# A four-layer linear-attention and MLP kernel: the first loads cut anew, two K projections split by weight halves, and a new order for the first layer

## The chip, the cores and the metric

The kernel runs on one core of a Trainium2 chip. The metric is the device time of one execution in microseconds. A page of the profile and a trace exist for one profiled execution, whose own time is given beside its span (first to last instruction of the program). All times inside the span are in microseconds from its start.

The engines are named as in the profile: PE is TensorE (matmuls and transposes; PEld is its weight load), ACT is ScalarE, DVE is VectorE, POOL is GpSimd, SP is SyncE, which issues the DMAs.

## The reference

Two kinds of layer run in turn, A, B, A, B, with the same weights both times. The sequence has 2048 tokens of width 512, in bfloat16.

```python
x = x + A(layernorm(x), wqkv, wo)   # 32 heads of 16
x = x + B(layernorm(x), w1, w2)     # 512 -> 1376 -> 512, relu
x = x + A(layernorm(x), wqkv, wo)
x = x + B(layernorm(x), w1, w2)

# A: linear attention
phi = lambda t: where(t > 0, t + 1, exp(t)) + 1e-6
pq, pk = phi(q), phi(k)
kv  = einsum("bhsd,bhse->bhde", pk, v);  z = pk.sum over s
num = einsum("bhqd,bhde->bhqe", pq, kv)
den = einsum("bhqd,bhd->bhq", pq, z) + 1e-6
A   = (num / den) @ wo
# B
B   = relu(x @ w1) @ w2
```

## The kernel before

The 2048 tokens are 16 tiles of 128, four tiles to a chunk. Every layer is written as a list of operations (`g.add`), each with its engine, what it reads and writes, and an assumed duration. A list scheduler in the kernel's own Python, `_list_schedule`, then fixes the order on each engine when the kernel is built. It takes the operations by priority: their place in the list, shifted by a table `HINTS`. The table `SEQS` forces the order of a few operations of the first layer on each engine, and `STT` names the steps that use a fused VectorE form. The engines run their lists strictly in order, with waits on semaphores, so the order is fixed and the chip decides only the times. PSUM banks (8) are also given out by the scheduler; an operation that takes a bank waits for the one that read it last.

The first layer, where all of the change lies, runs as follows. Names are those of the scheduler; `i` is a tile.

- SP issues the loads in this order: `ld_x0_0` (tile 0, 128 KB), `ld_x0_1` (tiles 1 to 3, 384 KB), `ld_wk0` and `ld_wk1` (the two halves of the K weights by contraction rows, 256 KB each), `ld_x1_0` (chunk 1, 512 KB), `ld_wq` (the Q weights, 512 KB), the chunks 2 and 3, then the V weights and `wo`.
- Warm-up: TensorE runs nine 512-column matmuls on zeros (`warm`, L451) and one of 256 columns (`warm2`, L454).
- Chunk 0: statistics `bnst`/`bnag` on VectorE (L476, L477); tile 3 has its mean and square sum from ScalarE (`mean_3`, `sq_3`, L890, L892). VectorE subtracts the mean (`cent`, L880). TensorE transposes the centred tile in four 128-column steps (`trp`, L549) and ScalarE or VectorE copies the result out of PSUM (`trev`, L553, L554). For tile 0 both are cut in halves (`trp0a`, `trp0b`). The division by the standard deviation is left to the evacuation of the projections (scale `rstd`, made on GpSimd: `veps`, `rstd`, L874, L876). `norm0` to `norm3` (L925) make the normalised tiles for the later K-transposed-x products.
- Chunk 1: statistics, `veps` and `rstd` for two tiles at a time, `norm4` to `norm7` (L515), transposes on TensorE (`trp4` to `trp7`).
- Chunks 2 and 3: the same, but transposed by DMA (`tr2_0`, `tr2_1`, `tr3_0`, L532).
- `kproj` is the K projection of one tile, four 512-column matmuls (one for each 128 rows of contraction); `qtok` is the Q projection of a tile of chunk 0, `qproj1_0` and so on those of the other chunks. Each is followed by `lin` and `exp` on ScalarE (L576, L578) and `em` and `phi` on VectorE (L580, L587; fused form L584). `g` are the products of K and normalised x, in 256 or 512 columns, which accumulate over all tiles. All of them are matmuls of L594.
- Then `zcol`, `kv` and `m` fold the V and output weights in; `den` (four matmuls of 32 output rows) gives the denominators, `lnd` and `rdc` their inverse on ScalarE, `spread` copies them out by DMA, `pqs` multiplies Q by them (L748), and `fin` is the output projection, with `resid` (L605) adding it to x.

In `a_k`, only tile 0's K projection is split by the two halves of its weights:

```python
for c0, n, key, tag in ((0, 2, "T0a", "a"), (2, 2, "T", "b")) if i == 0 and g.layer == 0 else ((0, 4, "T", ""),):
```

`FIRST_ORDER = (0, 3, 1, 2)` is the order in which the list has the tiles of chunk 0.

## Time and profile before

| | |
|---|---|
| median of 3 runs | 281.06 us (280.62 to 281.25) |
| the profiled execution | 281.25 us, span 279.5 us |
| PE busy | 275.4 us, 99% of the span |
| ACT, DVE, POOL busy | 172.5, 141.6 and 47.1 us |
| DMA | 22.62 MB, mean 81 GB/s over the span |
| first matmul (warm-up), first transpose, first K projection | 1.24, 5.05, 5.95 us |
| first transpose of chunk 1 | 13.68 us |

In the timeline, a row has the start, the time that the merged instructions span, the engine, the line, the operation, what it writes and reads, the shape and the count; in brackets stands the idle time before them and what ended it. Matmuls overlap in the array, so the spacing of starts, not the duration of one, is what a matmul costs. In the table by stretches, the columns are the stretch, its length, the busy time of PE, PEld, DVE, ACT and POOL (with the number of instructions), the granted clock, the busy share of the DMA engines and GB/s. In the chain, a row has the start and the length of a piece.

### The profile page before, as it was taken

To read this page: it belongs to the slowest core of one execution; us is meant where nothing else is said; L and a number is where in the kernel's file an instruction comes from. 1 tells how busy PE (TensorE), PEld (TensorE's weight loads), DVE (VectorE), ACT (ScalarE), POOL (GpSimd) and SP (SyncE) were. 2 spreads that over 40 slices of the span, in tenths; PEclk is the share of its full clock that TensorE was granted. 3 is DMA by queue.
4 is the path that set the end of the run, shared out by engine and by line. 5 is a ranking of instruction groups with operands and counts; after the bars stand their busy time and mean duration, and the time that the engine had idled before them with its cause. 6 is when DMAs were issued, how large, how long until landed. Compare 5 with 4: busy or idle time off the path is not lost.

```text
span 279.5 us, 4209 instructions
## 1 busy us (share of the span) xinstructions
PE 275.4 (99%) x1573; PEld 140.6 (50%) x1573; DVE 141.6 (51%) x381; ACT 172.5 (62%) x355; POOL 47.1 (17%) x126
## 2 busy tenths in 40 slices
PE   8999999999999999999999999999999999999996
PEld 3455656546554544544454455674554554454443
DVE  5899983899501362353353477379935300120222
ACT  4999797748864583578372799766884366226000
POOL 6500000044500170300040400003236100000000
PEclk9999999999999999999999999999999999999999
DMA  6913388654630053070004030075331641011012
GB/s 202 379 54 64 75 227 267 150 140 76 133 58 0 2 93 76 1 96 0 0 1 77 0 75 2 0 182 122 76 71 26 160 83 21 0 70 26 0 75 75
DMA packets 46356, 22.62 MB, mean 81 GB/s; under 512 B 36640, under 2 KB 44800, under 8 KB 46336
## 3 DMA queue, kind: packets, MB, share of 16 engines
q1 hardware_dynamic: 46336, 22.35, 33.9%
q8 instruction: 12, 0.20, 0.3%
q14 instruction: 8, 0.07, 0.1%
HBM read 7.14 MB, written 2.10 MB: 33 GB/s over the span
## 4 chain that ended last, share of the span: by engine, by line
PE 94%; DMA 2%; DVE 2%; SPq 1%; issue 0%
PE ps L594 94%; DMA xin<-in_A_x_dram 2%; DVE bst L476 1%; PE ps L549 0%; SPq L426 0%; SPq L420 0%; DVE xn L515 0%; DVE mv L477 0%; DVE xin L843 0%; DVE escr L580 0%; DVE veps L483 0%
## 5 line engine op out<-in xcount | busy, mean ns | idle before, releaser
L594 PE MATMUL ps<-w,big 128*128 128x512 bf16 (+3 forms) x363 | 77.5, 373 | 0.0
L594 PE MATMUL ps<-Tb,w 128*128 128x512 bf16 (+1 forms) x352 | 70.8, 360 | 0.0
L823 ACT ACTIVATE big<-ps 128x512 bf16<-128x512 f32 x71 | 42.3, 597 | 23.7 <-PE ps L594 23.4
L594 PEld LDWEIGHTS ps<-w,big 128*128 128x128 bf16 (+1 forms) x363 | 35.1, 98 | 41.2 <-ACT big L823 0.3
L594 PEld LDWEIGHTS ps<-Tb,w 128*128 128x128 bf16 x352 | 34.0, 98 | 32.8
L611 ACT ACTIVATE sqscr<-xres 128x512 bf16<-128x512 f32 x48 | 29.9, 625 | 31.1 <-DVE xres L605 30.8
L605 DVE SCALAR_TENSOR_TENSOR xres<-ps,xres 128x512 f32<-128x512 f32 x32 | 21.2, 690 | 42.6 <-PE ps L594 42.6
L602 DVE TENSOR_TENSOR xin<-ps,xres 128x512 bf16<-128x512 f32 x15 | 10.4, 691 | 49.7 <-PE ps L594 49.7
L576 ACT ACTIVATE big<-ps 128x512 bf16<-128x512 f32 x51 | 31.9, 628 | 5.0 <-PE ps L594 5.0
L594 PE MATMUL ps<-wqkv,Tb 128*128 128x512 bf16 x144 | 33.5, 381 | 0.0
L594 PE MATMUL ps<-big,xn 128*128 128x256 bf16 (+1 forms) x224 | 30.6, 288 | 0.0
L578 ACT ACTIVATE escr<-ps 128x512 bf16<-128x512 f32 x44 | 27.8, 636 | 1.0 <-PE ps L594 1.0
L594 PE MATMUL ps<-Tb,wqkv 128*128 128x512 bf16 x112 | 26.5, 379 | 0.0
L594 PEld LDWEIGHTS ps<-big,xn 128*128 128x128 bf16 x224 | 21.6, 98 | 8.6 <-issue 0.4
L594 PE MATMUL ps<-Mf,big 128*128 128x512 bf16 x112 | 25.2, 379 | 0.0
L580 DVE TENSOR_SCALAR escr<-escr 128x512 bf16<-128x512 bf16 x52 | 14.9, 293 | 18.0 <-ACT escr L578 17.7
L497 POOL TENSOR_SCALAR mean<-s 128x4 f32<-128x4 f32 x12 | 3.0, 247 | 119.0 <-DVE xres L605 118.8
L594 PEld LDWEIGHTS ps<-wqkv,Tb 128*128 128x128 bf16 x144 | 13.8, 98 | 16.0 <-ACT Tb L553 0.3
L587 DVE TENSOR_TENSOR big<-big,escr 128x512 bf16<-128x512 bf16 x49 | 20.5, 423 | 1.1
L524 ACT ACTIVATE xn<-xres,nbias,rstd 128x512 bf16<-128x512 f32 x15 | 12.0, 816 | 9.4 <-POOL nbias L509 9.4
L594 PEld LDWEIGHTS ps<-Mf,big 128*128 128x128 bf16 x112 | 10.8, 98 | 13.2 <-DVE big L748 0.5
L519 DVE TENSOR_SCALAR xn<-xres,mean,rstd 128x512 bf16<-128x512 f32 x23 | 15.2, 690 | 4.0 <-POOL nbias L509 3.9
(94 smaller groups left out, 226.2 us busy)
## 6 DMA issues: line engine op xcount, KB each, us to landing
big<-rdc SPq DMA_DIRECT2D x32, 128.0 KB, 2.7
xin<-in_A_x_dram SPq DMA_DIRECT2D x3, 512.0 KB, 8.1
w<-in_B_w_dram SPq DMA_DIRECT2D x1, 1376.0 KB, 8.3
w<-in_B_w_dram SPq DMA_DIRECT2D x1, 1280.0 KB, 10.9
wqkv<-in_A_wqkv_dram SPq DMA_DIRECT2D x2, 512.0 KB, 8.5
out_dram<-xin SPq DMA_DIRECT2D x2, 512.0 KB, 2.8
wqkv<-in_A_wqkv_dram SPq DMA_DIRECT2D x2, 256.0 KB, 3.8
wo<-in_A_wo_dram SPq DMA_DIRECT2D x1, 512.0 KB, 8.9
```

What stands on the lines that cost most here:

```text
L497: g.add(POOL, lambda e: e.tensor_scalar(mean[:, sl], s1[:, sl], -INV_D, None, ALU.mult), [("s1", i) for i in tl], [("mean", i) for i in tl ...
L519: ts = (POOL, lambda e: e.tensor_scalar(xn[:, i, :], src, mean[:, i:i + 1], rstd[:, i:i + 1], ALU.add, ALU.mult), C_POOL_NORM)
L524: (ACT, lambda e: e.activation(xn[:, i, :], src, ACTF.Identity, scale=rstd[:, i:i + 1], bias=nbias[:, i:i + 1]), C_ACT_SB_AP)],
L576: g.add(ACT, lambda e: e.activation(dst_ap, psv[:, b, :], ACTF.Identity, bias=1.0 + 1e-6, scale=sc), [("ps", b)] + rk, [dst_key], C_ACT_PS ...
L578: g.add(ACT, lambda e: e.activation(esc, psv[:, b, :], ACTF.Exp, scale=sc), [("ps", b)] + rk, [ekey], C_ACT_EXP + xd, name=name + "_exp")
L580: g.add(DVE, lambda e: e.tensor_scalar(esc, esc, 1.0, 1e-6, ALU.min, ALU.add), [ekey], [ekey], C_DVE_BF4X, name=name + "_em")
L587: g.add(DVE, lambda e: e.tensor_tensor(dst_ap, dst_ap, esc, ALU.max), [dst_key, ekey], [dst_key], 340.0, name=name + "_phi")
L594: last = e.matmul(o, l, r, start=st, stop=sp, skip_group_check=skip)
L602: g.add(DVE, lambda e: e.tensor_tensor(xin[:, i, :], psv[:, b, :], src, ALU.add), [("ps", b), skey], [("xin", i)], C_DVE_PSUM, name="resid ...
L605: g.add(DVE, lambda e: e.scalar_tensor_tensor(xres[:, i, :], psv[:, b, :], 0.0, src, ALU.add, ALU.add, accum_out=s1[:, i:i + 1]), [("ps", ...
L611: g.add(ACT, lambda e: e.activation(sqscr[:, q, :], xres[:, i, :], ACTF.Square, accum_out=s2[:, i:i + 1]), [("xres", i)], [("sqscr", q), ( ...
L823: g.add_flex([(ACT, lambda e, M=M, b=b, u=u: e.activation(unit_ap(u, M), psv[0:M, b, :], ACTF.Relu), C_ACT_PSUM), (DVE, lambda e, M=M, b=b ...
```

## The change

- The load of tiles 1 to 3 becomes two: tile 1 (128 KB), then tiles 2 and 3 (256 KB).
- The load of chunk 1 becomes two: tiles 4 and 5 (256 KB) ahead of the Q weights, tiles 6 and 7 behind them.
- The warm-up has eight matmuls instead of nine, and the 256-column one is gone.
- `FIRST_ORDER` is (0, 1, 3, 2), and the K projections of its first two tiles, 0 and 1, are split by the halves of their weights.
- `HINTS`, `SEQS` and `STT` are new for the first layer, and the scheduler assumes 218 ns for a group of denominators, and twice 95 ns more where it does not follow another one.

What the scheduler makes of it on TensorE, from the first transposes on:

```text
before: trp0a warm2 trp0b kproj0a trp3 trp2 kproj0b trp1 kproj3 kproj2 kproj1 qtok0 qtok3 qtok1
        trp4 trp5 qtok2 kproj4 trp6 trp7 kproj5 kproj6 kproj7 qproj1_0 qproj1_1 qproj1_2 qproj1_3 ...
after:  trp0a trp0b kproj0a trp3 trp2 trp1 kproj0b kproj2 kproj3 qtok0 qtok1 qtok3 qtok2
        trp4 trp5 kproj1a kproj1b kproj4 trp6 trp7 kproj5 kproj6 qproj1_1 kproj7 qproj1_0 qproj1_2 qproj1_3 ...
```

On VectorE, `bnst1` now stands ahead of `cent0`, and `trev2` and `trev1` come from ScalarE; on ScalarE, `trev3` stands ahead of `sq_3`, and `trev7` comes from VectorE in the place of `trev5`, which goes there. The denominators stand on TensorE as `den0 den2`, `den1`, `den3` before, each group between other matmuls, and as `den0`, `den2`, `den1`, `den3` after. `pqs1_3` follows `pqs1_2` directly on VectorE instead of standing behind `resid9`. The order of the later layers stays, but for the first matmul groups of the second layer, where `h0_0_0` now stands ahead of `hr0_1`. TensorE runs two matmuls fewer (one of the warm-up and the 256-column one); all else has the same number of them.

```diff
-    "dve": ["bnst0", "bnag0", "cent0", "bnst2", "bnst1", "bnag2", "cent3", "bnag1", "cent2", "trev0b"],
-    "act": ["mean_3", "trev0a", "sq_3", "trev3", "trev2", "trev1"],
-    "pool": ["veps_0", "rstd_0", "veps_2", "veps_1", "rstd_1", "var_3"],
-    "pe": ["trp0a", "warm2"],
+    "dve": ["bnst0", "bnag0", "bnst1"],
+    "act": ["mean_3", "trev0a", "trev3", "sq_3", "k0_exp", "k3_exp", "q0_0_lin", "k2_exp"],
+    "pool": ["veps_0", "rstd_0", "veps_2", "nm2_3"],
+    "pe": ["trp0a", "trp0b", "kproj0a", "trp2", "trp1"],
 }
-STT = {"0.k10", "0.k6", "0.k9", "0.q3_2", "0.q3_3"}
+STT = {"0.k13", "0.k5"}
...
         o.t_start = st
+        if o.key.startswith("0.den"):
+            o.dur = C_DEN if order[PE][-1].name.startswith("den") else C_DEN + 2 * C_MM_SWITCH
...
-                 WARM=9, SPLIT0=True, TAIL_SPLIT=True, LAST_HALVES=True, FIRST_PE_CHUNKS=2,
+                 WARM=8, SPLIT0=True, TAIL_SPLIT=True, LAST_HALVES=True, FIRST_PE_CHUNKS=2,
...
         ld_x(0, 0, 1, 100.0)
-        ld_x(0, 1, lat=1550.0)
+        ld_x(0, 1, 2, 550.0)
+        ld_x(0, 2, 4, 950.0)
...
-        ld_x(1, lat=1450.0)
-        dma(lambda e: e.dma_start(wqkv[:, :, 0:D], wq_v[:, :, 0:D]), [], [("wq",)], 1550.0, "ld_wq")
+        ld_x(1, 0, 2, 900.0)
+        dma(lambda e: e.dma_start(wqkv[:, :, 0:D], wq_v[:, :, 0:D]), [], [("wq",)], 1600.0, "ld_wq")
+        ld_x(1, 2, 4, 850.0)
...
-            g.add(PE, lambda e: e.matmul(psv[:, wt, 0:256], wrm[:, 0:128], wrm[:, 0:256], start=True, stop=True),
-                  [("wrm",)], [("ps", wt)], 213.0, name="warm2")
...
-            for c0, n, key, tag in ((0, 2, "T0a", "a"), (2, 2, "T", "b")) if i == 0 and g.layer == 0 else ((0, 4, "T", ""),):
+            for c0, n, key, tag in ((0, 2, "T0a" if i == 0 else "T", "a"), (2, 2, "T", "b")) if i in FIRST_ORDER[:2] and g.layer == 0 else ((0, 4, "T", ""),):
...
-        FIRST_ORDER = (0, 3, 1, 2)
+        FIRST_ORDER = (0, 1, 3, 2)
```

## The prediction

> **What bounds the kernel now.** I read the page first (busy time, then the chain), next the chain in order of time, then the timeline of each engine over the first 17 us, and last the DMA view narrowed to one issue at a time.

> ```profile
> PE 275.4 (99%) x1573; PEld 140.6 (50%) x1573; DVE 141.6 (51%) x381; ACT 172.5 (62%) x355; POOL 47.1 (17%) x126
> PE 94%; DMA 2%; DVE 2%; SPq 1%; issue 0%
> ```

> TensorE carries the chain, so a change pays only where TensorE starts later than it could, waits, or runs slowly. The chain names the one load that still sets a start:

> ```profile
> 2.69 6.34 DMA xin<-in_A_x_dram
> ...
> 13.31 0.33 DVE xn L515
> 13.64 0.04 issue
> 13.68 0.72 PE ps L549 x8
> ```

> Chunk 1 of x lands at 2.69 + 6.34 = 9.03; its statistics and norms lead to transposes `trp4` and `trp5` at 13.68. What TensorE did meanwhile (start, us, instructions):

> ```profile
> 5.05 0.42 PE L549 MATMUL ps<-ident,xn 128*128 128x128 bf16 x2
> 5.26 0.42 PE L454 MATMUL ps<-wrm 128*128 128x256 bf16 x1
> 5.48 0.42 PE L549 MATMUL ps<-ident,xn 128*128 128x128 bf16 x2
> 5.95 0.84 PE L594 MATMUL ps<-wqkv,Tb 128*128 128x512 bf16 x2
> 6.73 0.72 PE L549 MATMUL ps<-ident,xn 128*128 128x128 bf16 x8
> 7.30 0.59 PE L594 MATMUL ps<-wqkv,Tb 128*128 128x512 bf16 x2
> 7.73 0.39 PE L549 MATMUL ps<-ident,xn 128*128 128x128 bf16 x4
> 7.95 5.34 PE L594 MATMUL ps<-wqkv,Tb 128*128 128x512 bf16 x24
> 13.68 0.72 PE L549 MATMUL ps<-ident,xn 128*128 128x128 bf16 x8 [0.39 <-DVE xn L515]
> ```

> The nine warm-up matmuls stand 0.43 us apart; at 5.95 a 512-column matmul still takes 0.40; from 7.30 on it is 0.216 ((5.34 - 0.38)/23). The 24 at 7.95 would hand over at 7.95 + 24 x 0.216 = 13.13; the next start is 13.68, so chunk 1 costs 0.55. From there to 277.1 TensorE is dense. The wait list of its matmuls has 0.4 us beside the start, so nothing else large can be won.

> **The change, part by part.** All times below are of the profiled execution: 281.25 with a span of 279.5 (1.75 outside it). The runs' median is 281.06, 0.19 lower.

> *Start.* One warm-up matmul (0.43) and the filler (0.21) go: TensorE is free at 1.24 + 8 x 0.427 = 4.65. VectorE now does `bnst1` ahead of `cent0`: 3.65 + 0.08 + 0.58, so `cent0` runs at 4.33 and ends at 4.68 (it was 3.87 to 4.22). Tile 1's load is the 128 KB issued second at 1.25; with the 2.1 us of the first load it lands at 3.36, in time. Transposes: 4.74 to 5.17, four at 0.107. ScalarE's `mean_3` starts when tiles 2 and 3 are in (512 KB as before; 4.45 to 4.6) and holds ScalarE 0.63, so `trev0a` starts at 5.2 and ends at 5.6; `kproj0a` starts 0.06 later, at 5.67 instead of 5.95, if `wk0` is in. `wk0` landed at 1.71 + 3.6 = 5.3 with the same bytes ahead; one more issue (0.47) makes it 5.3 to 5.6. Two matmuls at 0.40, then three transposes (`trp3`, `trp2`, `trp1`, 0.22 each; VectorE has the last centred tile at about 6.2) and `kproj0b` (0.43): `kproj2` starts at 7.60. In the old order the same work was over at 7.95: 0.35 gained. `trev2` moves to VectorE, 7.15 to 7.56, just in time.

> *Between 7.6 and chunk 1.* Before, 4 K projections and 3 Q projections ran ahead of `trp4`; now `kproj1` goes behind it and `qtok2` ahead of it: the same count. `kproj2` and `kproj3` end at 7.60 + 8 x 0.216 = 9.33; then `qtok0` wants the Q weights. These landed at 3.20 + 7.27 = 10.47, just ahead of their use at 10.54. Now 256 KB of chunk 1 go behind them. How early that makes them depends on a dip of the loads:

> ```profile
> 5.50:6.50 1.00, 0.95 (x5) 0.26 (x3) 0.81 (x4) 0.99 (x3) 0.00 (x0) 1.00 0.98 240
> 6.50:7.50 1.00, 1.00 (x11) 0.56 (x10) 0.97 (x5) 0.33 (x2) 0.89 (x3) 1.00 0.76 284
> ...
> 9.00:10.50 1.50, 1.50 (x8) 0.59 (x6) 1.45 (x4) 1.50 (x4) 0.52 (x1) 1.00 1.03 414
> ```

> (The last column is GB/s.) Late end: the dip stays, 262 KB at 414 GB/s are 0.63, so 9.84; with a little for shorter rows 9.9. Early end: the two slow stretches run at about 390, as 7.5 to 9 did, which is 0.26 MB or 0.65 us more: 9.2. No row decides, since the dip stands where the 4 KB rows of chunk 1 begin and these become 2 KB; I take the middle, 9.55. TensorE then waits 0.21 at `qtok0`, and the 16 matmuls of four Q projections end at 9.55 + 3.45 = 13.0, against 13.68: 0.68 gained (0.33 at the late end, 0.89 at the early one).
> [...]

> *Is chunk 1 ready by 13.0?* Its first half lands by 8.4 and its second half by 10.5 to 10.6 (the byte place that the Q weights had). VectorE: `bnst6`, `bnst7` 10.63 to 11.82, `norm4` 11.9 to 12.3, `norm5` to 12.6. `rstd4` on GpSimd needs 0.8 after `veps4` at about 10.4. So `trp4` is ready 0.7 ahead, `trp5` too (its 0.09 wait of the old order goes), and `kproj1` between `trp5` and `kproj4` covers `trev4` (0.5 on ScalarE). The stall of 0.55 is gone; late next is the Q weights.

> *13 to 44 us.* ScalarE was idle 0.17 us between 14.4 and 29.6, so TensorE's bank waits hang on it. Its list there changes little: two transposes' evacuations fewer and one more (0.49 each), `sq_3` (0.61) moved from idle time at 5.8 to behind `trev3`. Laying its operations end to end (0.57 with a scale per token, 0.48 without) against TensorE at 0.216, each release comes 0.2 to 0.6 us ahead of need; the thinnest are `q1_0_exp` before `g0_3_0` and `q0_3_lin` before `kproj8`. `tr3_0` leaves about 1 us later than at 29.35, but `kproj12` comes at 35 instead of the old first use at 33.7. Three steps fewer use the fused VectorE form, so ScalarE has three more `lin` (0.48 each): one between 26 and 38, where it idles 0.8, 0.5 and 0.65, and two (`q3_2`, `q3_3`) between 45 and 52, where it idles 0.4, 0.3 and 1.1. I cost this at nothing; if the cover fails, each late release costs its own lateness.

> *Denominators.* Entering and leaving the 32-column matmuls costs about 0.1 each way:

> ```profile
> 45.18 0.40 PE L594 MATMUL ps<-xres,Zc 128*32 128x512 bf16 x4
> 45.41 0.39 PE L594 MATMUL ps<-big,Zc 128*32 128x512 bf16 x4
> 45.73 0.62 PE L594 MATMUL ps<-GT,wqkv 128*128 128x128 bf16 x8
> ```

> The second group starts 0.23 after the first, the one after it 0.31 later. `den0` and `den2` stood together (three blocks of denominators); now all four stand alone: 0.20 lost. Later `pqs1_3` no longer stands behind `resid9` (0.61) on VectorE, so the 0.14 that `fin4` waited at 60.5 goes. Layers 1 to 3 keep their order but for one pair at 67.9.

> Sum: 0.68 + 0.09 + 0.14 - 0.20 = 0.71, so 281.25 - 0.71 = 280.54. The median run stands 0.19 below the profiled one; part of that is likely a shorter stall at 13.68, so I take half: **280.45**.

> **The rivals.**
> (a) *The Q weights take over the stall.* At the late end (9.9) the gain is 0.33 + 0.09 + 0.14 - 0.20 = 0.36: 280.9, or 280.7 beside the median run. For it: the weights were only 0.07 ahead before. Against: in a run with less of the dip both waits shrink.
> (b) *The clock comes late: slower.* Full rate came about 5.2 us after the first matmul, between 5.95 and 6.73. The old order kept TensorE nearly busy till then (pause 5.69 to 5.95). The new one pauses 5.17 to 5.67, without the filler. If that pause restarts the count, full rate comes at 5.67 + 5.2 = 10.9; 4.4 us at half rate lose 2.2, and the wait for the Q weights vanishes under it: 281.25 - 0.92 + 2.2 = 282.5. It decides for slower if full rate comes later than about 9.1. Against: the old pause did no visible harm.
> [...]
> (c) *Something on the way to the matmuls is late*, above all ScalarE: if its four thinnest margins fail by 0.3 each, 1.2 is lost: 281.7. The dense 13.7 to 44.5 under an equally full ScalarE speaks against it.
> (d) *All is early*: Q weights at 9.2, no wait: 281.25 - 0.92, 280.3.

> **How the numbers follow.** About 0.2% (0.56 us) is what a measurement of this kernel can tell from no change: faster means below 280.5. The forecast with (d): 0.48, ending at 280.0 to 280.5. (a): 0.24, within 0.2%. (b): 0.15 and (c): 0.13, slower. The range takes in the forecast, (a), (d), (c) and the cheaper half of (b): 279.9 to 282.0.

> **What would show it.** Right: 512-column matmuls 0.216 apart by 7.2; `kproj0a` near 5.7; no idle time before L554 at about 13.0; idle time, if any, before `qtok0` with a release by the wqkv load. Wrong: matmuls 0.43 apart after 7, TensorE waiting on ScalarE between 14 and 30, or `trp4` still waiting for a norm at 13.7.

## The result, and the profile after

The changed kernel takes 282.31 us (median of 6 runs, 281.92 to 282.98), the kernel before beside it 280.95 (6 runs, 280.62 to 281.49): ratio 1.0049, interval 1.0032 to 1.0066. It is 1.36 us slower, 1.9 above the forecast and 0.3 outside the range. The profiled execution took 282.64 with a span of 280.9, so 1.4 more inside the span than the profiled one of before.

The first part of the loss lies in the timeline of TensorE at the start (columns as before; the lines of the code are five to seven higher than in before):

```profile
3.77 1.06 PE L458 MATMUL ps<-wrm 128*128 128x512 bf16 x2
4.73 0.61 PE L554 MATMUL ps<-ident,xn 128*128 128x128 bf16 x4
6.01 1.03 PE L599 MATMUL ps<-wqkv,Tb 128*128 128x512 bf16 x2 [0.68 <-ACT Tb L558]
6.83 1.49 PE L554 MATMUL ps<-ident,xn 128*128 128x128 bf16 x12
8.12 6.50 PE L599 MATMUL ps<-wqkv,Tb 128*128 128x512 bf16 x26
14.45 0.61 PE L554 MATMUL ps<-ident,xn 128*128 128x128 bf16 x8
```

The first transposes start at 4.73 (forecast 4.74), but `kproj0a` starts at 6.01, not 5.67, behind an evacuation by ScalarE. Twelve transposes from 6.83 to 8.12 are 0.107 apart, against 0.055 for the four from 7.73 to 7.95 in before: the array is still at half rate (the first entry of the clock record stands at 9.58). `trp4` starts at 14.45, which is 0.77 later than in before; no wait stands ahead of it any more. `trp5`'s wait of 0.09 is gone too, so 0.67 is carried into the dense stretch.

The denominators follow each other no longer:

```profile
45.94 0.40 PE L599 MATMUL ps<-xres,Zc 128*32 128x512 bf16 x4
46.27 0.29 PE L599 MATMUL ps<-GT,wqkv 128*128 128x128 bf16 x2
46.39 2.78 PE L599 MATMUL ps<-big,xn 128*128 128x256 bf16 x24
49.11 0.40 PE L599 MATMUL ps<-big,Zc 128*32 128x512 bf16 x4
49.44 0.61 PE L599 MATMUL ps<-big,xn 128*128 128x256 bf16 x4
```

From its start each block of four takes 0.33 (45.94 to 46.27, 49.11 to 49.44), about 0.1 of it for leaving (one block followed the other after 0.23 in before, 45.18 to 45.41). Set against before, TensorE is 0.205 later behind the denominators than ahead of them: the forecast said 0.20. At `fin4` it wins back 0.15 (forecast 0.14). From 61 to 177 us it stays 0.72 late.

The rest of the loss was not in the forecast at all. In the chain of waits, and in the list of what TensorE waited for, a DMA transpose in the second attention layer appears that before does not have:

```profile
199.52 3.70 DMA Tb<-xn
203.22 0.05 issue
203.26 75.23 PE ps L599 x415
```

```profile
PE ps L599 <- ACT Tb L558: 0.7, 1, 0.7
PE ps L599 <- DMA Tb<-xn: 0.5, 1, 0.5
```

In before the same group of 96-column matmuls starts without a wait, at 201.88:

```profile
201.88 0.50 PE L594 MATMUL ps<-w,Tb 128*128 128x96 bf16 x8
```

It stands 0.87 behind the group ahead of it (201.01), which starts at 201.73 in after. Here it would be due at 202.60 and starts at 203.26: 0.66 lost, in a layer that the change does not touch. 0.72 + 0.66 = 1.38.

### The profile page after: what moved, and what is told of

The parts are those of the page before. It is cut to its first block, busy times and chain, and to the rows that moved or that the text cites. A ratio compares the mean times of both kernels' runs of the same rounds, so it can differ in the third digit from the quotient of the medians.

```text
span 280.9 us, 4212 instructions
## 1 busy us (share of the span) xinstructions
PE 276.1 (98%) x1571; PEld 141.1 (50%) x1571; DVE 140.9 (50%) x382; ACT 173.0 (62%) x357; POOL 46.7 (17%) x126
## 4 chain that ended last, share of the span: by engine, by line
PE 93%; DMA 2%; DVE 2%; POOL 1%; ACT 0%; issue 0%; SPq 0%; POOLq 0%
PE ps L599 92%; DVE xres L610 1%; DMA Tb<-xn 1%; DMA xin<-in_A_x_dram 1%; PE ps L554 1%; POOL rstd L512 0%; DVE xn L524 0%; SPq L425 0%; ACT sqscr L895 0%; POOL nbias L514 0%; POOL mean L502 0%; DVE big L753 0%; DVE xin L848 0%; ACT Tb L558 0%; POOL veps L510 0%
## 5 line engine op out<-in xcount | busy, mean ns | idle before, releaser
L828 ACT ACTIVATE big<-ps 128x512 bf16<-128x512 f32 x72 | 42.7, 596 | 24.5 <-PE ps L599 24.5
L581 ACT ACTIVATE big<-ps 128x512 bf16<-128x512 f32 x54 | 33.6, 625 | 4.9 <-PE ps L599 4.7
L607 DVE TENSOR_TENSOR xin<-ps,xres 128x512 bf16<-128x512 f32 x15 | 10.4, 690 | 49.7 <-PE ps L599 49.7
L599 PE MATMUL ps<-wqkv,Tb 128*128 128x512 bf16 x144 | 34.4, 388 | 0.7 <-ACT Tb L558 0.7
L529 ACT ACTIVATE xn<-xres,nbias,rstd 128x512 bf16<-128x512 f32 x15 | 11.9, 814 | 8.8 <-POOL nbias L514 8.8
```

The costliest lines, as they stand in the source:

```text
L529: (ACT, lambda e: e.activation(xn[:, i, :], src, ACTF.Identity, scale=rstd[:, i:i + 1], bias=nbias[:, i:i + 1]), C_ACT_SB_AP)],
L581: g.add(ACT, lambda e: e.activation(dst_ap, psv[:, b, :], ACTF.Identity, bias=1.0 + 1e-6, scale=sc), [("ps", b)] + rk, [dst_key], C_ACT_PS ...
L599: last = e.matmul(o, l, r, start=st, stop=sp, skip_group_check=skip)
L607: g.add(DVE, lambda e: e.tensor_tensor(xin[:, i, :], psv[:, b, :], src, ALU.add), [("ps", b), skey], [("xin", i)], C_DVE_PSUM, name="resid ...
L828: g.add_flex([(ACT, lambda e, M=M, b=b, u=u: e.activation(unit_ap(u, M), psv[0:M, b, :], ACTF.Relu), C_ACT_PSUM), (DVE, lambda e, M=M, b=b ...
```

## The experiments

Where an order is to stay, an edit leaves every other place: moves of single steps and the joining of loads are made behind the scheduler, and added steps left the order of the rest as it was in the traces. All times are medians; the ratio is to the runs of before on the same chip. The table has what the traces show of each profiled execution: the moment of the full clock (first entry of the clock record), the landings of the second half of the K weights and of the Q weights (issue plus time to landing in the DMA view, which is given to 0.1), the start of `trp4`, and how much longer than in before the stretch from 177 us to the last matmul took.

| kernel | full clock | wk1 | wq | `trp4` | late at 202 | median us |
|---|---|---|---|---|---|---|
| before, four executions | 6.46, 4.29, 5.15, 5.72 | 6.18, 7.68, 6.38, 6.48 | 10.50, 10.40, 9.20, 9.80 | 13.68, 13.63, 12.84, 13.11 | 0 | 280.61 to 280.95 |
| after, two executions | 9.58, 5.88 | 7.45, 7.75 | 10.17, 10.47 | 14.45, 14.03 | 0.67, 0.92 | 282.31, 282.30 |
| e1_fill | 5.76 | 7.75 | 9.88 | 13.49 | 0.68 | 282.05 |
| e7_a10 | no entry | 7.15 | 9.57 | 13.05 | 0.57 | 282.02 |
| e10_a14 | 4.46 | 7.35 | 9.68 | 13.21 | 0 | 281.64 |
| e11_fill14 | 6.28 | 8.15 | 10.37 | 13.89 | 0 | 281.31 |
| e4_one, e4_again | 6.93, 7.18 | 6.48, 6.78 | 9.50, 9.50 | 13.30, 13.24 | 0 | 280.79, 280.86 |
| e13_nofill | 5.91 | 6.98 | 9.40 | 12.94 | 0 | 281.00 |
| e6_b8 | 6.85 | 6.68 | 9.50 | 13.13 | 0.10 | 281.18 |
| e12_pqs | 3.93 | 5.98 | 9.50 | 12.96 | 0 | 280.54 |
| e5_den, e8_best, e9_den2 | 5.82, 5.18, 5.96 | 8.88, 7.98, 6.88 | 11.10, 10.90, 9.00 | 16.35, 14.44, 12.80 | 0.17, 0.15, 0.18 | 281.58, 281.41, 282.60 |

**Both kernels again.**

> The changed kernel once more, nothing edited. Two theories for its 1.36 us. First: the pause of TensorE between the first transposes and the first K projection (0.88 us in its trace, 0.26 in the trace of before) makes the full clock come 3.1 us later, worth 0.7 to 0.9 us at the first transpose of chunk 1, and a stall of 0.67 us at 202.5 us, where TensorE waits for the DMA transpose of the second layer, is the rest. If both belong to the order, a second profile shows full rate again between 9 and 10 us and the wait at about 202.5 us again, and about 282.3 us. Rival: the stall, or the moment of the clock, belongs to that one execution; then one of them is missing here, with a time about 0.7 lower for the profiled execution. [...]

> The kernel before once more, nothing edited. If the moment of the full clock follows from TensorE's own activity, it comes between 6.2 and 6.7 us again and the first transpose of chunk 1 starts at 13.6 to 13.8; 281.0 us. If it moves by itself from run to run, full rate comes up to 3 us later here and 512-column matmuls are still 0.43 us apart at 8 us; the wait for chunk 1 (0.55 us) then hides up to 1.1 us of the half rate. No wait at 201 to 203 us is expected in this order; if there is one, that stall has nothing to do with the change.

After: 282.30 (ratio 1.0054, 1.0035 to 1.0073). Before: 280.96 (1.0003, 0.9986 to 1.0020). The stall at 202 us is there again in after (0.92) and absent in before, so it belongs to the kernel. The clock does not: it came at 5.88 in this execution of after instead of 9.58, and at 4.29 instead of 6.46 in before (the records fit windows of 3.41 us, as the next experiment shows). Still `trp4` starts at 14.03 in this execution of after, since the loads were late: `kproj0b` waited until 7.90 with the K weights landing at 7.75, and the Q weights came at 10.47. The medians of before here, 280.96 and the 280.65 of the runs that it is compared with, are one kernel on one chip: a step of 0.3 us is not told by the times alone.

**The pause of TensorE filled.** After `trp0b`, four matmuls on zeros:

```diff
+ g.add(PE, lambda e: [e.matmul(psv[:, wt, 0:256], wrm[:, 0:128], wrm[:, 0:256], start=True, stop=True)
+                      for k in range(4)][-1], [("wrm",)], [("ps", wt)], 0.1, name="fill")
```

> The changed kernel with four 256-column matmuls on zeros (0.85 us at half rate) in the pause between the second pair of transposes of tile 0 and the first K projection; same order otherwise. Theory pause: full rate comes near 6.5 us instead of 9.6, the first K projection stays at 6.0, and the first transpose of chunk 1 starts at about 13.5 to 13.6 instead of 14.45 (the Q weights at 10.13 now set it): 0.85 less, about 281.45 if the stall at 202.5 us stays, 280.8 if not. Rival: it was the missing ninth warm-up matmul or the phase of a window, not the pause: full rate stays at 9.6 and the time at 282.3. Rival: the loads set the start, so the time is 282.3 even at full clock.

282.05 (1.0038, 1.0021 to 1.0055). Full rate at 5.76, `trp4` at 13.49 as foreseen, the stall as before. But the median moved by 0.25 only, not 0.85, and 0.25 is no more than before differs from itself: the late clock is not there in every execution of after. The traces say why. In sixteen of them the record of the full clock lasts 273.07 or 276.48 us, which is 80 or 81 times 3.413 (in e5_den it is broken once, into 3.41 and 269.65, 1 and 79 times; in e7_a10 there is none). So the records fit windows of 3.41 us, and their place against the kernel is another each time: the first entry stands between 3.93 and 9.58. The view by stretches, cut along the windows ahead of the first entry (the columns are those of the table by stretches in the prediction; the clock column has no entry to show yet and reads 1.00), after first, then its repeat:

```profile
2.75:6.16 3.41, 2.73 (x10) 0.93 (x9) 3.00 (x10) 0.99 (x3) 1.47 (x6) 1.00 0.90 269
```

```profile
2.47:5.88 3.41, 2.89 (x10) 0.95 (x8) 2.76 (x9) 1.04 (x4) 1.68 (x6) 1.00 0.91 260
```

The first window of after holds all of the pause, and the full clock did not follow it; the window of the repeat, 0.28 earlier, holds a little less of it, and the full clock did. Counting each matmul by the time it takes at half rate (512 columns in 0.427 us, the spacing of the warm-up matmuls in after, no tails), the two are 2.43 and 2.56 us busy. Over 17 executions of all these kernels, every window at whose end the clock became full had at least 2.56 of 3.41 us (75%, again_after), and the fullest ahead of one had 2.52 (74%, e4_again, from its first matmul to 3.77). With that bound, and all places of the window alike, an estimate from the traces of the two first executions: after gets its full clock later than 7.3 us in 38% of the executions, and at 6.8 us in the mean; before never later than 7.2, and at 5.5 in the mean. It holds for loads that land as they did there: in again_before tiles 1 to 3 landed at 5.22 instead of 4.43, and TensorE paused for 1.1 us in the order of before too.

**Tiles 1 to 3 in one load again.** With `cent0` ahead of `bnst1` on VectorE and two filler matmuls; chunk 1 stays in two loads.

```diff
+ merge("0.ld_x0_1", "0.ld_x0_2", lambda e: e.dma_start(xin[:, 1:4, :], tok_view(A_x, 0, 1, 4)))
+ move(DVE, "0.cent0", "0.bnst1")
```

`merge` puts the load of tiles 1 to 3 in the place of the first of the two and takes the second out; `move` puts `cent0` ahead of `bnst1`. The edit adds the two fillers as well, in the way of e1_fill.

> The changed kernel with tiles 1 to 3 in one load again (chunk 1 still in two around the Q weights), the centring of tile 0 ahead of the statistics of tile 1 on VectorE, and two 256-column matmuls on zeros behind the first transposes; all other orders as in the changed kernel. Theory: the extra load issue pushed tiles 2 and 3 to 4.94 and every later load by about 0.45 us. Here tiles 1 to 3 land at 4.4, the first K projection starts at 5.5 to 5.6 instead of 6.01, the Q weights land at 9.6 to 9.8 instead of 10.13, full rate comes near 6.5, and the first transpose of chunk 1 starts at 13.1 to 13.3: 1.2 less than the changed kernel, about 281.1 with the stall at 202.5 us and 280.45 without. Rival: bytes set the landings, not issues; then the Q weights stay at 10.1, the transposes start at 13.6, and the time is that of the kernel with the filler alone.

> The kernel with tiles 1 to 3 in one load and two filler matmuls once more, since its first time (280.79, the same as before) rests on loads that landed early in the profiled execution. If its gain over the changed kernel is real it stands at 280.7 to 281.1, with no wait at 202 us and the second transpose issued 0.05 us after its wait on SP. If the landings of that execution made it, the time is nearer to 281.5.

280.79 (0.9995, 0.9978 to 1.0012) and 280.86 (1.0003, 0.9983 to 1.0023): 1.5 faster than after, the same as before. No wait at 202 us, the Q weights at 9.50 both times, `trp4` at 13.30 and 13.24. So the third load issue seems to cost on two sides: later weights at the start, and the stall at 202. Here it is undone together with the place of `cent0`; the two were not tried apart.

**Without the two filler matmuls of that kernel.**

> The kernel with one load for tiles 1 to 3, without the two filler matmuls. Theory: TensorE pauses for 0.4 to 0.8 us at 5.1 us; a window of 3.41 us that holds the whole pause and other gaps is then not counted as busy in some executions, full rate comes 3.4 us later in these, and the median is 0.1 to 0.3 above that with the fillers (280.8). Rival: the pause is short enough for every window; then 280.8 again.

281.00 (1.0008, 0.9993 to 1.0023), beside 280.8: no difference that counts. The pause is some 0.45 us in its trace, and by the bound above, which is an estimate, no place of the window misses with it: it would take 0.87 us without work inside one window (3.41 - 2.54, between 2.52 and 2.56). This kernel differs from after by the joined load and the place of `cent0` alone, and its interval lies clear below that of after (1.0035 to 1.0073): nearly all of the loss comes with these two.

**Where the stall at 202 comes from.** The V row's load in three, in before (two loads of SP more, no order changed), and in after (two and six more):

```diff
- dma(lambda e: e.dma_start(wvl[:], A_wqkv[D - 1:D, 2 * D:3 * D].broadcast_to([128, D])), ...
+ for k, (a, b) in enumerate(((0, 172), (172, 342), (342, 512))):
+     dma(lambda e, a=a, b=b: e.dma_start(wvl[:, a:b], ...
```

> The kernel before with the small load of the last V row cut in three by columns: SP issues two loads more, as in the changed kernel; no order on any other engine changes, and the V row is not waited for. Theory position: the stall at 202 us comes from SP's place in its own program. The three kernels with eight first loads lost 0.40 us on SP between the wait and the second of the two DMA transposes at 198 to 199 us (0.45 instead of 0.05), and the transpose landed 0.9 late; here the same gap of about 0.45 us appears at about 198.4 us, the transpose lands at 202.0 to 202.5 instead of 201.5, TensorE waits 0.3 to 0.7 us at 202 us, and the time is about 0.5 us above the kernel before. Rival: the stall comes from the later arrival or the order of the first layer; then there is no gap on SP, no wait at 202 us, and the time of the kernel before.

> The changed kernel with the small load of the last V row cut in three: SP issues two loads more still, ten instead of eight of the first ones counted so. Theory position: the gap of 0.4 us on SP stands at a fixed place of its program, so it moves to an earlier instruction of the kernel, before the first of the two DMA transposes or in the copies ahead of it, where SP has slack; the second transpose is issued 0.05 us after its wait, the wait of TensorE at 202 us is gone or under 0.2 us, and the time falls by 0.5 to 0.7 us to about 281.7. Rival count: every load issued early makes the later transposes slower; then the stall stays or grows, 282.3 or more.

> The changed kernel with the small load of the last V row cut in seven: six loads of SP more than the changed kernel. Two more had moved the gap of 0.45 us on SP from between the two DMA transposes of 198 us to before the first, where it still delayed both. Theory position: six more move it ahead of them into the copies of the denominators or into SP's idle time, both transposes are issued within 0.05 us of their waits, TensorE does not wait at 202 us, and the time is 0.5 to 0.9 below the changed kernel: 281.5 to 281.8. What then remains over the kernel before is the start. Rival: the transposes are late for another reason, and 282.3 stays.

281.18 (1.0006, 0.9987 to 1.0026), 282.02 (1.0042, 1.0021 to 1.0064) and 281.64 (1.0032, 1.0007 to 1.0057). Only the last came as expected: in e6_b8 the hole is there but TensorE waits 0.09, not 0.3 to 0.7, and in e7_a10 the wait stays, 0.57. The view of the tile `Tb` gives, for the two transposes of SP near 198 us, the duration of each (ns) and the start of the first and the last. In the order before, after, e6_b8, e7_a10, e10_a14:

```profile
L532 SPq DMA_TRANSPOSE Tb<-xn x2: 1239/1250/1261, 197.1 to 198.4; - x2
```

```profile
L537 SPq DMA_TRANSPOSE Tb<-xn x2: 1232/1434/1635, 197.8 to 199.5; - x2
```

```profile
L534 SPq DMA_TRANSPOSE Tb<-xn x2: 1238/1243/1248, 196.0 to 197.7; - x2
```

```profile
L539 SPq DMA_TRANSPOSE Tb<-xn x2: 1237/1288/1340, 196.7 to 198.1; - x2
```

```profile
L539 SPq DMA_TRANSPOSE Tb<-xn x2: 1250/1261/1272, 196.5 to 197.9; - x2
```

The starts stand 1.35 apart in before (197.05 and 198.40 in the trace), 1.75 in after and in e6_b8, which has the order of before but as many issues on SP as after, 1.44 in e7_a10 and 1.35 in e10_a14. The 0.40 is a hole on SP: from the end of a wait to the transpose behind it 0.45 pass instead of 0.05. Counting the instructions of SP that the trace shows, waits too, it stands ahead of the 80th in every kernel where that is an issue that does not have to wait for long. In after and e6_b8 the 80th is the second transpose; in e7_a10 it is the first (wait over at 196.20, issue at 196.67); in e10_a14 it is the second of four copies of the denominators, issued at 191.32, 0.46 behind the end of the one ahead of it, where SP has time to spare. In e4_one, with one issue fewer than after, it is the next transpose, for which SP waits 3 us anyway. So the hole goes with SP's place in its own program: shown. What makes it stays open. An 8 KB load of instructions starts 0.6 to 0.7 after the issue behind the hole in after, e6_b8 and e7_a10 (200.19, 198.43, 197.28) and 1.25 after it in e10_a14 (192.57); whether the two belong together was not tried.

The hole is only part of the stall. In before the second transpose lands 3.15 after its issue and 0.34 ahead of need. In after it lands 3.7 after it:

```profile
DMA to landing us min/median/max: 3.1/3.4/3.7
```

(after; before has 3.1/3.2/3.2, e10_a14 3.2/3.3/3.3.) So 0.40 from the hole and 0.55 from the longer landing, less the 0.34 in hand, make 0.61 of the 0.66. In e6_b8 it took 3.4, and the pair was issued 0.29 earlier against TensorE than in before (4.25 instead of 3.96 ahead of the matmuls that start at 201.01 there), so that almost nothing was left to wait for. With after's order the longer landing came and went with the hole (3.7 to 3.9 in four executions with it at the transposes, 3.3 in e10_a14 and e11_fill14). But the hole is not what makes it long: e5_den, e8_best and e9_den2 have landings of 3.6 with their transposes 1.34 apart, e5_den as follows.

```profile
L537 SPq DMA_TRANSPOSE Tb<-xn x2: 1233/1250/1268, 200.2 to 201.5; - x2
DMA to landing us min/median/max: 3.3/3.4/3.6
```

The cause of the longer landing stays open. With both gone, after is 0.66 faster (281.64 against 282.30, on two chips; 0.6 by their ratios to before), as its two traces had priced it (0.67 and 0.92).

**Pause and hole both taken away.**

> The changed kernel with the four filler matmuls in the pause of TensorE and the six more loads of SP: both suspected causes taken away, loads of tile 1 and of chunk 1 as in the changed kernel. The filler alone gave 0.25 us. Theory: 281.2 to 281.5, so that what is left over before (some 0.5 us) is the later landing of the K and Q weights, which the kernel with one load for tiles 1 to 3 (280.8) does not have. Rival: pause and stall are all of it; then 280.7 to 280.9, as the forecast had it.

281.31 (1.0017, 1.0000 to 1.0034), 0.33 below e10_a14 and 0.5 above the kernel with one load for tiles 1 to 3. In its trace the second half of the K weights landed at 8.15, and `kproj0b` had to wait 0.7 for it.

**Was there something to win in before?**

> The kernel before a third time, for its profile alone. Question: the forecast valued the wait of 0.55 us for chunk 1 at 13.68 us as it stood in one profiled execution (281.25), while the runs of before have their median at 280.6 to 280.8. Theory: in the median execution chunk 1 lands earlier than 9.03 us, as it did at 8.1 us in the kernel with only two more small loads (first transpose of chunk 1 at 13.13), so that wait is mostly absent and there was little to win. Then some of the profiles of before show the transpose at 13.1 to 13.3 and a time of 280.4 to 280.7. Rival: the wait is there always and the spread of times lies elsewhere; then the transpose starts at 13.6 to 13.7 every time.

> The kernel before a fourth time, for the same question: first transpose of chunk 1 at 13.1 to 13.3 us in some executions (theory: landings vary by about 1 us from execution to execution), or at 13.6 to 13.7 in all (rival).

280.14 and 280.62 (one run each). TensorE in the first of them:

```profile
7.43 0.39 PE L549 MATMUL ps<-ident,xn 128*128 128x128 bf16 x4
7.66 5.34 PE L594 MATMUL ps<-wqkv,Tb 128*128 128x512 bf16 x24
12.84 0.61 PE L549 MATMUL ps<-ident,xn 128*128 128x128 bf16 x8
```

7.66 + 24 x 0.216 = 12.84: no wait for chunk 1. Nor is there one in the second (7.93 and 13.11). The load of chunk 1 took this long from its issue at 2.69, in the profiled execution of before and in b_third:

```profile
xin<-in_A_x_dram SPq DMA_DIRECT2D x1, 512.0 KB, 6.3
```

```profile
xin<-in_A_x_dram SPq DMA_DIRECT2D x1, 512.0 KB, 5.1
```

So the wait of 0.55 that the forecast removed is one execution's. In the other three it is not there: twice chunk 1 landed early, and once (again_before) TensorE itself ran 0.5 late, with the second half of the K weights at 7.68. Nor is it there in e6_b8 and e12_pqs, which start in the order of before (`trp4` at 13.13 and 12.96): one execution of six. The times follow: 281.25 and 281.19 where `trp4` starts at 13.6 or later, 280.14 and 280.62 where it does not.

**`pqs1_3` ahead of `resid9`, alone, in before.**

> The kernel before with one move: the multiplication pqs1_3 stands ahead of resid9 on VectorE. Theory: the output projection that waited 0.14 us at 60.5 us in the profile of before no longer waits, and the end comes 0.14 us earlier: 280.5 beside 280.65, which is below what the times can tell, so the trace decides. Rival: resid9, now later by 0.35 us, delays the bank of a later projection and takes the 0.14 back.

280.54 (0.9997, 0.9978 to 1.0016): the same. In the trace `fin4` follows without a gap, and TensorE gains 0.15 there on the profiled execution of before. But b_third gains the same 0.15 without the edit: this wait too comes and goes.

**The denominators.** In the kernel with one load for tiles 1 to 3, `"0.den1": 50` instead of 191 puts `den1` behind `den0`, and the scheduler moves other steps of the first layer with it; e8_best adds three moves at the start, e9_den2 keeps `mev1`, the evacuation of the second product with the output weights, on ScalarE. `m2` is the third of these products.

> The kernel with tiles 1 to 3 in one load and two filler matmuls (280.79 before), and the denominators den1 planned directly behind den0, so that three blocks of 32-column matmuls are entered instead of four; the scheduler moves two later steps of the first layer with it. Theory: each block costs 0.2 us in entering and leaving, so the end of the first layer comes 0.2 us earlier and the time falls to 280.6. Rival: the switch is hidden or comes back as a wait of the first output projection for the scaled Q, and the time stays at 280.8 or above.

> The kernel with one load for tiles 1 to 3, two filler matmuls and den1 behind den0, and three small moves at the start: VectorE centres tile 3 ahead of the statistics of tile 2 and normalises tile 0 behind the two evacuations, TensorE transposes tile 1 ahead of tile 2. Theory: the second half of the first K projection waited until 7.67 us for the last transposes and their evacuation; here it starts at 7.3 to 7.4, and the first transpose of chunk 1 at about 13.0 if the Q weights land by 9.5, at 13.3 if they land at 9.9: 280.3 to 280.6. Rival: the Q weights set it in most executions, and the time is that of the kernel without the moves, 280.6.

> As the kernel with den1 behind den0, but the evacuation of the second output-weight product kept on ScalarE, so that two output projections stand between the last V product and m2 again. Theory: the earlier try lost 0.53 us at m2, which waited for the masked V product that den1 had covered, and so hid the 0.2 us of the block of denominators saved. Here no wait stands before m2, and the kernel is 0.2 us faster than the one with four separate blocks: 280.6 beside 280.8. Rival: another wait of the first layer takes the 0.2.

281.58 (1.0019, 0.9999 to 1.0039), 281.41 (1.0018, 0.9998 to 1.0037) and 282.60 (1.0070, 1.0046 to 1.0093): the medians are all above 280.8, e9_den2's clear of noise. The block saved is paid back at once, first in e5_den and then in e9_den2:

```profile
55.96 0.60 PE L601 MATMUL ps<-wo,KVT 128*128 128x512 bf16 x2 [0.53 <-DVE KVT L682]
```

```profile
56.27 1.04 PE L601 MATMUL ps<-Mf,big 128*128 128x512 bf16 x4 [1.27 <-DVE big L755]
```

In the kernel without the move, `den1` and one output projection stand between the V products and `m2` and cover the masking on VectorE; in e5_den neither does. In e9_den2 the output projection `fin4` comes two places earlier and waits for its `pqs1_3`. The three moves of e8_best show nothing: in its trace the K weights landed at 7.98 and TensorE waited 0.94 for them. No kernel tried beats before by what can be measured.

## Why the prediction was wrong

Three steps of the sum failed: the start was to come 0.35 earlier and came later, the wait of 0.55 that was to be removed is not there in most executions, and the later layers were put at nothing and cost 0.66.

*Start (0.35 earlier): failed.* `kproj0a` came at 6.01, not 5.67, and at 5.87 to 6.25 in the other five executions with tile 1 loaded alone. The step took tiles 2 and 3 "4.45 to 4.6"; they landed at 4.91 and 4.91 in after, 4.51 to 4.61 in the rest. The K weights' first half, put at 5.3 to 5.6, landed at 5.67 to 5.88: the old landing and the whole of one issue, 5.31 + 0.47, would have given 5.78. The second half was not in the sum at all. It landed at 6.18 in the first execution of before and came at 7.15 to 8.15, middle 7.6, with tile 1 alone; in the twelve executions with one load for tiles 1 to 3 the middle is 6.7. The one more issue of 0.47 ahead of it is half of that difference; the rest stays open, and before too had it at 7.68 once. Put at 13.0, `trp4` started between 13.05 and 14.45 in these six executions, two of them with the pause filled, middle 13.7; in the six with the start of before the middle is 13.1.

*Q weights (9.55, 9.2 to 9.9): failed at the late end.* In the six executions with tile 1 alone and chunk 1 cut they landed at 9.57 to 10.47, middle 10.0. What the late end has for shorter rows (9.84 to 9.9) was the author's estimate; no run shows it alone. And the 10.47 they were measured against was a late one: the order of before has 9.20 to 10.50, middle 9.65, with 256 KB more ahead of them. With tiles 1 to 3 in one load and chunk 1 cut it is 9.00 to 11.10, middle 9.5. By these middles, cutting chunk 1 around them brought 0.15 and the third small load took 0.5; beside ranges of 0.9 to 2.1 us that is a hint and no more.

*The stall at 13.68 (0.55, of 0.68 gained): right in its execution, wrong as the kernel's.* The wait list of one profiled execution was taken for what every run pays. The forecast saw that the median lay 0.19 lower and gave half of that to this stall; the repeats show it absent in three of four, where TensorE has nothing to win from an earlier chunk 1, and the median of before beside the later kernels is 280.6 to 280.8. Of the sum of 0.71, some 0.4 (three quarters of 0.55) was not there to win.

*Rival (b), the late clock: it did come late, but not by a count that restarts, and the price was wrong.* The profiled execution did run at half rate, until 9.58, but its repeat, with the same order, until 5.88. The traces fit windows of 3.41 us, of which at least 2.56 were busy where the clock became full at the end; so, by the estimate above, a pause of 0.9 us costs a whole window in 38% of the executions and nothing in the others. The forecast set the pause at 0.5, and held against it that the pause of before, which is 0.26, did no harm. Filling it moved the medians by 0.25 and 0.33, each within noise, and not by 2.2: where the loads are late, TensorE waits at full rate instead (0.7 for the K weights in e11_fill14, with the full clock from 6.28). That its 282.5 is near the result is chance, since half of the loss is the stall at 202. Nor does any run show a price for the cheaper half of (b), at which the range ends (282.0); what the runs showed are the 0.25 and 0.33.

*Middle, rival (c): the cost of nothing held.* Between 14 and 44 us TensorE is busy without a break in after too (30.00 of 30.00 us), with ScalarE at 27.04 instead of 25.84.

*Denominators, `trp5`, `fin4`: confirmed* (0.205, 0.09, 0.15), `fin4` for such executions as have its wait.

*"Layers 1 to 3 keep their order": true and not enough.* The order stayed, and 0.66 was lost there all the same, through the hole of 0.40 that SP's longer program brought between the two transposes and through a landing longer by 0.55, whose cause is open. The prediction counted what each queue issues in the first layer, not what stands behind it.

Put together from the medians: 0.66 (the late transpose, after to e10_a14), 0.33 (the pause, to e11_fill14), 0.5 (tile 1 loaded alone and its statistics ahead of `cent0`, to e4), and 0.1 to 0.25 that the rest stands above before, within its interval. That is 1.6 to 1.7, the distance from 282.30 to the medians of before beside these kernels, and not the 1.36 of the first comparison. Each step is about as large as the intervals, so the split rests on the traces more than on the times. The stall at 202 is shown, and that nearly all of the loss comes with the third load and the place of `cent0`; how the loss at the start divides between late weights, late tiles and the clock is not.

## What to carry to other kernels

Profile the kernel before two or three times before pricing a wait for a load: a wait that comes and goes with the landings is worth its mean. Count what an extra DMA issue does to everything behind it on its queue, to the end of the program, and look for the transposes or copies with the least time in hand there. At the start of a kernel keep TensorE's pauses short against the windows of its clock (3.41 us in these traces; with a pause of 0.88 the full clock came as late as 9.58), and fill them if they grow; and before work is moved to join others of its kind, look at what it had been covering.

## What the runs showed of the hardware

```profile
2.41:5.82 3.41, 3.41 (x13) 1.42 (x12) 2.79 (x7) 1.24 (x4) 1.88 (x6) 1.00 0.88 269
5.82:9.23 3.41, 1.49 (x15) 0.80 (x14) 1.99 (x8) 1.21 (x3) 2.76 (x8) 1.00 0.96 316
9.23:12.64 3.41, 3.41 (x9) 1.21 (x8) 3.01 (x10) 1.95 (x3) 0.83 (x2) 0.50 1.04 399
```

A window with 1.49 us busy lost it. Windows with 2.67 (again_after, 5.88 to 9.29), 2.31 (e10_a14, 4.46 to 7.87) and 1.97 kept it, the last in again_before:

```profile
4.29:7.71 3.42, 1.97 (x17) 0.95 (x16) 2.47 (x9) 1.65 (x6) 1.38 (x5) 1.00 0.98 296
7.71:11.12 3.41, 3.41 (x23) 1.76 (x22) 2.82 (x8) 3.41 (x7) 2.05 (x6) 1.00 1.04 399
```

So these traces put the loss between 1.49 and 1.97 us busy in one window, from one loss alone. The first loads landed very unevenly: the second half of the K weights, issued at 2.18 in the twelve executions with one load for tiles 1 to 3, landed between 5.98 and 8.88. And SP lost some 0.4 us ahead of the 80th instruction that its trace shows, in after and e6_b8 the second transpose near 198 us, in e7_a10, with two issues more than after, the first (196.20 to 196.67), in e10_a14, with six more, a copy of the denominators (issued at 191.32): issues put in ahead moved it to an earlier step.
